# A transformer block's head and attention: last x tile on another queue, crossbar transposes, fewer fillers, a new order

## The chip, the cores and the metric

The kernel runs on one core of one Trainium2 chip. The metric is the device time of one execution in microseconds. Executions vary, so each kernel is run several times in alternation with the kernel before, on the same chip; the calls used three chips (the record's numbers 6, 8 and 14), so fast means of different calls are compared with care. An execution is called slow when it is more than 1.5% above the fastest of its kernel; verdicts use the fast ones only. The profile's span is shorter than the measured time by about 1.8 us in every run listed here (98.78 us and 97.0, 101.95 and 100.1; the extremes are 1.74 and 1.88), so spans can be compared with times once 1.8 us is added. The granted clock is the share of full speed that the profile records for TensorE. A load's landing is the moment at which its data has arrived; it is issued earlier, from the queue of an engine.

## The reference

B = 2 batches of N = 256 tokens, width D = 1152, everything in bf16:

```python
mod = (silu(c) @ w_mod).reshape(B, 6, 1, D)      # the kernel needs shift_a, scale_a, gate_a
h   = layernorm(x) * (1 + scale_a) + shift_a
q, k, v = split(h @ wqkv)
p   = softmax(q @ k.T * D ** -0.5)
out = x + gate_a * ((p @ v) @ wo)
```

## The kernel before

The 512 tokens are four x tiles of 128 rows, x0 to x3. The rows of x0 and x1 (batch 0) are transposed first and centred afterwards, with means from a matmul with ones; x2 and x3 are normalised first. Keys are computed from the scaled, not yet shifted rows as soon as the scale weights (s0 to s3, column groups of `w_mod`) and the first chunks of the key weights (w0 to w8) are there. A helper records every operation with what it reads and writes and adds the semaphores; each engine is given its operations in the order of the list. Fillers are matmuls on zeros whose results nobody uses; they are meant to keep TensorE busy at the start. The parts that the change touches:

```python
SGROUPS = [(0, 2), (2, 4), (4, 6), (6, 9)]
LOADS = [                       # all on SyncE's queue
    ('s', 0), ('w', 0, 1), ('s', 1), ('w', 1, 2), ('w', 2, 4), ('s', 2), ('w', 4, 6), ('s', 3), ('w', 6, 9),
]
WARM = 12                       # filler matmuls on zeros, 128x512, ahead of everything on TensorE
ORDER = [                       # head: the emission order of some 80 steps on all engines
    ('bn', 2, 1), ('third', 2, 0), ('cT',), ...
]
...
    op(AC, lambda e: e.dma_start(c_sb[:, :], c[:, :]), w=[("c",)], dma=True)
    load_x(SP, 2)
    load_x(AC, 3)
    load_x(SP, 0)
    load_x(AC, 1)               # the last x tile: second on ScalarE's queue
...
    def p_T(b):                 # probabilities transposed on TensorE, 4 per batch
        bank = next_bank()
        for qt in range(2):
            i = 2 * b + qt
            for sbk in range(2):
                op(PE, lambda pe, ...: pe.transpose(psb[bank][...], e_sb[:, i, sbk * P:(sbk + 1) * P], ident[:, :]), ...)
        op(DVE, lambda v: v.tensor_copy(pT_sb[:, b, :, :], psb[bank][...]), ...)
...
    v_tile(0)
    sbanks = [score(i) for i in range(TT)]
    for i in range(TT):
        softmax(i, sbanks[i])
    v_tile(1)
    ...                         # gate row, and 8 DMAs that spread it over the partitions
    v_tile(2)
    p_T(0)
    p_T(1)
    v_tile(3)
```

## Time and profile before

| | before |
|---|---|
| time, median of the first runs | 100.17 us (100.02 to 100.8, 4 runs) |
| the profiled execution | 101.95 us, span 100.1 us, mean granted clock 0.983, state slow |
| TensorE busy | 94.0 us |
| x1's landing | 8.95 us |
| first key matmul | 13.91 us |
| third set of scale matmuls (needs s3) | 22.61 us |

The second row is the one to keep in mind. The profile is of one execution, and this one was slow. The rest of the table describes that execution, not the median. The last row is this piece of its chain of waits (start, length, what), with which later runs are compared:

```profile
22.61 0.65 PE psbank L490 x27
```

### The profile page before, as it was taken

To read this page: it belongs to the slowest core of one execution; us is meant where nothing else is said; L and a number is where in the kernel's file an instruction comes from. 1 tells how busy PE (TensorE), PEld (TensorE's weight loads), DVE (VectorE), ACT (ScalarE), POOL (GpSimd) and SP (SyncE) were. 2 spreads that over 40 slices of the span, in tenths; PEclk is the share of its full clock that TensorE was granted. 3 is DMA by queue.
4 is the path that set the end of the run, shared out by engine and by line. 5 is a ranking of instruction groups with operands and counts; after the bars stand their busy time and mean duration, and the time that the engine had idled before them with its cause. 6 is when DMAs were issued, how large, how long until landed. Compare 5 with 4: busy or idle time off the path is not lost.

```text
span 100.1 us, 1901 instructions
## 1 busy us (share of the span) xinstructions
PE 94.0 (94%) x770; PEld 58.4 (58%) x776; DVE 49.2 (49%) x139; ACT 28.6 (29%) x63; POOL 12.8 (13%) x36
## 2 busy tenths in 40 slices
PE   5974989999999999999999999999999999999990
PEld 1344978855564454544445687556667865665670
DVE  1258196254199641320840246650523655799571
ACT  1854567980123200000604033351103810000000
POOL 4004363348021030210000000000000000000000
PEclk9996699999999999999999999999999999999999
DMA  2999999999999999999999910003775755221222
GB/s 31 356 329 318 358 326 340 359 327 313 351 351 346 355 322 386 385 393 388 395 388 391 369 51 0 0 0 17 27 51 45 40 45 62 80 79 39 79 79 79
DMA packets 20092, 21.65 MB, mean 216 GB/s; under 512 B 882, under 2 KB 16114, under 8 KB 20084
## 3 DMA queue, kind: packets, MB, share of 16 engines
q1 hardware_dynamic: 19792, 20.94, 72.0%
q10 hardware_dynamic: 292, 0.59, 1.6%
q8 instruction: 6, 0.10, 0.4%
q14 instruction: 2, 0.02, 0.0%
HBM read 19.76 MB, written 1.18 MB: 209 GB/s over the span
## 4 chain that ended last, share of the span: by engine, by line
PE 87%; DMA 7%; DVE 2%; ACTq 1%; issue 1%
PE psbank L542 35%; PE psbank L720 18%; PE psbank L845 18%; DMA x_sb<-in_x_dram 7%; PE psbank L807 4%; PE psbank L733 4%; PE psbank L490 3%; PE psbank L408 2%; PE psbank L392 2%; PE psbank L784 1%; ACTq L295 1%; DVE pvT_sb L521 1%; DVE nm_sb L417 0%; PE psbank L767 0%; DVE xnT_sb L426 0%
## 5 line engine op out<-in xcount | busy, mean ns | idle before, releaser
L542 PE MATMUL psbank<-pvT_sb,wq_sb 128*128 128x512 bf16 (+2 forms) x107 | 18.2, 319 | 0.3
L720 PE MATMUL psbank<-wq_sb,hT_sb 128*128 128x384 bf16 x108 | 18.2, 326 | 0.0
L542 PE MATMUL psbank<-hT_sb,wq_sb 128*128 128x512 bf16 x79 | 17.9, 379 | 0.1
L845 PE MATMUL psbank<-wm_sb,pvT_sb 128*128 128x384 bf16 x99 | 16.3, 326 | 0.0
L720 PEld LDWEIGHTS psbank<-wq_sb,hT_sb 128*128 128x128 bf16 x108 | 10.4, 98 | 7.0 <-DVE v_sb L337 0.2
L542 PEld LDWEIGHTS psbank<-pvT_sb,wq_sb 128*128 128x128 bf16 x111 | 9.7, 98 | 6.9 <-DVE pvT_sb L521 0.3
L845 PEld LDWEIGHTS psbank<-wm_sb,pvT_sb 128*128 128x128 bf16 x99 | 9.7, 98 | 6.3
L542 PEld LDWEIGHTS psbank<-hT_sb,wq_sb 128*128 128x128 bf16 x81 | 7.8, 97 | 9.1
L339 ACT ACTIVATE qkT_sb<-psbank 128x512 bf16<-128x512 f32 x8 | 4.3, 598 | 22.3 <-PE psbank L542 22.3
L337 DVE CAST qkT_sb<-psbank 128x512 bf16<-128x512 f32 x10 | 6.3, 685 | 5.6 <-PE psbank L542 5.6
L337 DVE CAST v_sb<-psbank 128x384 bf16<-128x384 f32 x6 | 3.2, 554 | 10.4 <-PE psbank L720 10.4
L858 DVE TENSOR_TENSOR ga_sb<-psbank,gate_rep 128x384 bf16<-128x384 f32 x11 | 6.1, 556 | 4.0 <-PE psbank L845 4.0
L331 PE MATMUL psbank<-warm_sb 128*128 128x512 bf16 x12 | 4.6, 568 | 1.2 <-DVE warm_sb L319 1.2
L339 ACT ACTIVATE v_sb<-psbank 128x384 bf16<-128x384 f32 x6 | 2.9, 487 | 9.8 <-PE psbank L720 9.8
L490 PEld LDWEIGHTS psbank<-scT_sb,wm_sb 128*128 128x128 bf16 x162 | 5.0, 96 | 1.0
L490 PE MATMUL psbank<-scT_sb,wm_sb 128*128 128x2 bf16 x162 | 5.0, 163 | 0.0
L484 DVE TENSOR_TENSOR hT_sb<-pvT_sb,rep_sb 128x256 bf16<-128x256 bf16 x9 | 3.2, 421 | 2.7 <-ACT rep_sb L478 2.7
L343 DVE BATCH_NORM_STATS2 stat_sb<-x_sb 128x6 f32<-128x384 bf16 x4 | 2.0, 553 | 4.4 <-DMA x_sb<-in_x_dram 4.4
L861 DVE TENSOR_TENSOR xo_sb<-x_sb,ga_sb 128x384 bf16<-128x384 bf16 x11 | 3.9, 358 | 0.4
L733 PE MATMUL psbank<-qkT_sb 128*128 128x256 bf16 x36 | 4.1, 273 | 0.0
L807 PE MATMUL psbank<-pT_sb,v_sb 128*128 128x256 bf16 x36 | 4.1, 273 | 0.0
L392 PE MATMUL psbank<-ident,x_sb 128*128 128x128 bf16 x18 | 2.0, 266 | 2.1 <-DMA x_sb<-in_x_dram 1.6
(86 smaller groups left out, 89.0 us busy)
## 6 DMA issues: line engine op xcount, KB each, us to landing
wm_sb<-in_w_mod_dram SPq DMA_DIRECT2D x4, 864.0 KB, 9.4
wq_sb<-in_wqkv_dram SPq DMA_DIRECT2D x4, 672.0 KB, 10.0
wq_sb<-in_wqkv_dram SPq DMA_DIRECT2D x3, 864.0 KB, 11.5
wm_sb<-in_w_mod_dram SPq DMA_DIRECT2D x1, 2592.0 KB, 16.5
wm_sb<-in_wo_dram SPq DMA_DIRECT2D x1, 2592.0 KB, 18.2
wm_sb<-in_w_mod_dram SPq DMA_DIRECT2D x3, 576.0 KB, 8.2
wq_sb<-in_wqkv_dram SPq DMA_DIRECT2D x2, 576.0 KB, 10.3
out_dram<-xo_sb SPq DMA_DIRECT2D x11, 96.0 KB, 1.6
```

The source lines that it names most:

```text
L331: op(PE, lambda pe: pe.matmul(ps[bank][:, 0:512], warm_sb[:, 0:P], warm_sb[:, 0:512], start=True, stop=True), r=[("warm",)], w=[("ps", bank)])
L337: op(DVE, lambda v: v.tensor_copy(dst, src), r=r, w=w)
L339: op(AC, lambda a: a.activation(dst, src, ACT.Copy), r=r, w=w)
L392: op(PE, lambda pe, cc=cc, bank=bank, lo=lo, src=src: pe.transpose(psb[bank][:, lo:lo + P], src[:, i, cc * P:(cc + 1) * P], ident[:, :]), ...
L490: op(PE, lambda pe, cc=cc, k=k: pe.matmul(ps[7][:, col + 2 * cc:col + 2 * cc + 2], src[:, k, (cc - base) * P:(cc - base + 1) * P], scT_sb[ ...
L542: op(PE, lambda pe: pe.matmul(ps[bank][:, lo:hi], wq_sb[:, k, col * P:(col + 1) * P], src[:, k, lo:hi], start=(k == 0) if start is None el ...
L720: op(PE, lambda pe, k=k, q=q, bank=bank: pe.matmul(ps[bank][:, 0:384], hT_sb[:, k, i * P:(i + 1) * P], wq_sb[:, k, 2 * D + q * 384:2 * D + ...
L733: op(PE, lambda pe, cc=cc: pe.matmul(ps[bank][:, 0:NTOK], qkT_sb[:, cc, i * P:(i + 1) * P], qkT_sb[:, DC + cc, b * NTOK:(b + 1) * NTOK], s ...
L807: op(PE, lambda pe, h=h, cc=cc, sbk=sbk: pe.matmul(ps[bank][:, h * NTOK:(h + 1) * NTOK], v_sb[:, 2 * b + sbk, cc * P:(cc + 1) * P], pT_sb[ ...
L845: op(PE, lambda pe, i=i, k=k, rhs=rhs, n=n, bank=bank: pe.matmul(ps[bank][:, 0:n], pvT_sb[:, k, i * P:(i + 1) * P], rhs, start=(k == 0), s ...
L858: op(DVE, lambda v, b=b, c0=c0, c1=c1, n=n, bank=bank, s=s: v.tensor_tensor(ga_sb[:, s, 0:n], ps[bank][:, 0:n], gate_rep[:, b, c0:c1], ALU ...
L861: op(DVE, lambda v, i=i, c0=c0, c1=c1, n=n, s=s: v.tensor_tensor(xo_sb[:, i, c0:c1], x_sb[:, i, c0:c1], ga_sb[:, s, 0:n], ALU.add), r=[("x ...
```

## The change

The intent: x1 joins the other x tiles at the front of SyncE's queue and so lands before the weights; TensorE's eight transposes of the probabilities become four crossbar DMAs; 12 fillers become 5 + 4; and the order of the head is recomputed for the new landing times.

```diff
 LOADS = [
-    ('s', 0), ('w', 0, 1), ('s', 1), ('w', 1, 2), ('w', 2, 4), ('s', 2), ('w', 4, 6), ('s', 3), ('w', 6, 9),
+    ('x', 0), ('x', 1), ('s', 0), ('s', 1), ('w', 0, 1), ('w', 1, 2), ('w', 2, 4), ('s', 2), ('w', 4, 6),
+    ('s', 3), ('w', 6, 9),
 ]
-WARM = 12
+WARM = 5
 ORDER = [
-    ('bn', 2, 1), ('third', 2, 0), ('cT',), ('third', 2, 1), ('bn', 3, 0), ('xT', 0, 1), ...
+    ('cT',), ('third', 2, 0), ('cTo',), ('bn', 2, 0), ('e1',), ('third', 2, 1), ('warm', 4), ('d1',), ...
     (the other steps, and where ('smm', 1) stands: now ahead of the first key matmul)
 ]
     load_x(SP, 2)
     load_x(AC, 3)
-    load_x(SP, 0)
-    load_x(AC, 1)
-    def p_T(b):
-        ... (four TensorE transposes and a copy)
+    def p_T(i):
+        b, qt = i // 2, i % 2
+        op(SP, lambda e: e.dma_start(pT_sb[:, b, :, qt * P:(qt + 1) * P], e_sb[:, i, :], transpose=True),
+           r=[("e", i)], w=[("pT", b, qt)], dma=True)
     for i in range(TT):
         softmax(i, sbanks[i])
+        p_T(i)
     v_tile(2)
-    p_T(0)
-    p_T(1)
```

## The prediction

> **What bounds the kernel now.** I began with the chain of waits that ends last, because it says which engine's time the end is made of.
>
> ```profile
> PE 87%; DMA 7%; DVE 2%; ACTq 1%; issue 1%
> ...
> 1.70 7.25 DMA x_sb<-in_x_dram
> 8.95 0.04 issue
> 8.99 1.14 PE psbank L392 x9
> 10.13 0.96 PE psbank L408 x9
> ...
> 13.34 0.52 DVE pvT_sb L521
> 13.86 0.05 issue
> 13.91 1.00 PE psbank L542 x10
> ...
> 71.47 0.45 PE psbank L767 x8
> ...
> 97.85 0.29 DVE xo_sb L850
> ```
>
> The columns are start, length and what. From 13.91 us, the first key matmul, to 97.8 us the chain is TensorE with gaps of at most 0.05 us. Before 13.91 it is one load, an x tile of 288 KB that takes 7.25 us, and then 4.96 us of work that this tile releases. So time can be won in two ways: let the first key matmul start earlier, provided that what it then needs is there, or take instructions off TensorE.
>
> Next I asked why that tile is late, in the DMA issues and then line by line, narrowed to one issue at a time.
>
> ```profile
> x_sb<-in_x_dram SPq DMA_DIRECT2D x2, 288.0 KB, 3.9
> x_sb<-in_x_dram ACTq DMA_DIRECT2D x2, 288.0 KB, 6.1
> ```
>
> The single issues are: x2 issued at 0.73, 3.1 us to landing (3.8); x0 1.18 + 4.8 = 6.0; x3 1.30 + 4.9 = 6.2; x1 1.70 + 7.3 = 9.0. x1 is second on ScalarE's queue, while SyncE's queue already carries the first scale weights s0 (576 KB, issued at 1.65, landed at 9.2). Further landings, needed below: the key weights w0 2.11 + 7.8 = 9.9, s1 2.78 + 8.9 = 11.7, w1 3.27 + 9.1 = 12.4, s2 7.47 + 8.2 = 15.7, s3 10.69 + 9.0 = 19.7.
>
> Last, the stretches with the granted clock, since filler matmuls are removed.
>
> ```profile
> core 0: us, PE busy (x) PEld busy (x) DVE busy (x) ACT busy (x) POOL busy (x), PEclk, DMA share, GB/s
> 1.20:5.00 3.80, 3.80 (x9) 1.32 (x10) 0.63 (x2) 2.42 (x4) 0.62 (x4) 1.00 0.82 254
> 5.00:8.40 3.40, 1.92 (x22) 1.01 (x20) 2.18 (x7) 1.96 (x10) 0.00 (x0) 1.00 1.06 333
> 8.40:11.80 3.40, 2.81 (x27) 2.81 (x28) 1.49 (x5) 1.67 (x4) 2.06 (x5) 0.51 1.08 335
> 13.90:20.70 6.80, 6.71 (x91) 5.66 (x94) 4.00 (x14) 5.36 (x10) 3.04 (x7) 1.00 1.08 348
> ```
>
> DMA runs at about 340 GB/s throughout, and TensorE's clock falls to half from 8.4 to 11.8, after a stretch in which it was busy 1.92 of 3.40 us. In that half-clock stretch a transpose or a mean matmul starts every 0.107 us (0.96 us for 9).
>
> [...]
>
> **The change, part by part.**
>
> 1. *x1 on SyncE, ahead of the weights.* Its queue becomes x2, x0, x1, s0, s1, w0; ScalarE's keeps c and x3. The four tiles are 4 x 0.295 = 1.18 MB. The stretches moved 35 KB in the second microsecond, then 212, 385, 335, 323 and 333 KB, so 1.18 MB have gone by at about 5.7 us. x0 and x3 landed about 1.3 us after their 0.885 MB had passed (4.8 against 6.0 to 6.2). With the same lag x1 lands at 7.0, 2 us earlier. The price is w0: w1 has the same bytes ahead of it as before (12.4), w0 stands 0.229 MB / 0.34 MB per us = 0.7 us ahead of w1, so 11.7 instead of 9.9, and s1 about 11.0. The first key matmul cannot start before 11.7.
>
> 2. *The new order of the head.* It has no fewer real instructions, only another order, so I walked each engine with before's durations. ScalarE: both statistics of x3 until 7.6, eviction of x0's second part 0.70 to 8.3, Ln and Exp to 8.8, eviction of x1's second part to 9.5. VectorE: eviction of x1's first part to 8.15, x2 normalised 8.85 to 9.6. TensorE: x1 transposed 7.05 to 7.6, three parts of the means, 18 scale matmuls when s0 is there (9.2), x2's transposes, the last mean. At full clock that mean ends at 10.65; then ScalarE scales it (0.3), VectorE centres (0.42) and scales (0.35), and the second 18 scale matmuls end at 11.65: first key matmul at 11.8. At half clock from 8.45 to 11.86, as in the trace of before, the last mean ends at 11.7 and the first key matmul comes at 12.85. I take the middle, 12.3.
>
> 3. *After it.* 18 scale matmuls (0.43 us) stood behind the first key matmul in before and now stand ahead of it. The block of the first four key chunks ended at 20.67, 6.76 after its start; it needs 6.3 now. So it ends at 12.3 + 6.3 = 18.6: 2.1 us gained (2.6 at full clock, 1.5 at half). Is the rest fed? s2 (15.7) is wanted at about 17.3. s3 (19.7) was wanted at 22.6 and is now wanted at about 20.1 to 20.5. Both are there; before's slack at s3, 2.9 us, is the cap of what the head can give. Later weights had over 3 us of slack.
>
> 4. *Fillers.* 12 become 5 + 4. Those cost no path time in before (the chain was waiting for x1); they matter for the clock alone.
>
> 5. *Crossbar transposes.* Eight PE transposes leave the chain: 0.45 us. Two VectorE copies (0.76 us) go too, beside other work. In their place are four DMAs of 64 KB. The last probabilities are scaled at 66.2 and the first use is at 76.1; both move earlier together. A regular small DMA here takes 4.8 to 9.2 us under a queue of eight (the gate rows) and 1.6 us alone (the stores), so about 7 us of slack should do. They stand ahead of the gate rows in SyncE's queue, which begin at 67.5.
>
> Sum: 2.1 + 0.45 = 2.55 us off 100.29 = 97.75; with full clock 2.6 + 0.45 gives 97.2, with half clock 1.5 + 0.45 gives 98.3.
>
> **Rivals.**
>
> *The clock takes the gain.* Fewer fillers leave the stretch around 5 to 8.4 emptier still (perhaps 1.5 of 3.4 us), so the half-clock stretch stays[...]. For it: before lost its clock at 1.92 of 3.40. Against: with x1 at 7.0 TensorE is nearly always busy from then on[...]. Cost: result 98.3[...].
>
> *Weights become the bound.* w0 at 11.7 replaces x1 as the last wait. For it: s1 was moved ahead of w0. It is already in my sum as the floor 11.7; if DMA order costs 0.5 us more, the result is 98.2.
>
> *The transposes stall SyncE.* If one takes 4 us to issue, the four end 4 or 5 us after the gate rows should have begun; those in before landed between 72.3 and 84.8, and the second batch's are wanted by VectorE at 87.0. That slack of 2 us would be spent, result about 99 to 101. Against: no view shows SyncE busy then; it had waited 24 us for the gate rows' source. I give it one chance in twelve.
>
> *The head is hidden anyway.* Then only 0.45 us remain: 99.8. Against: the chain of waits has no idle TensorE after 13.91 that could absorb an earlier start.
>
> **Range and chances.** The two clock cases give 97.2 and 98.3, and x1's landing is uncertain by 0.4 us; that makes 96.9 to 98.9, with 97.8 in the middle, rounded towards the half-clock case. The 2% mark is at 98.3, right at the unlucky clock case, so faster by over 2% gets 0.66, within 2% 0.30, slower by over 2% 0.04 for stalled transposes.
>
> **What would show it.** Right: x1's landing about 7 us; the first key matmul between 11.8 and 12.9 with its last wait on VectorE's scaling or on w0; the fourth chunk's end near 18.6; no PE group for the probabilities' transposes, and the product with v following the last v tile without a gap. Wrong: a wait of TensorE on a weight DMA near 15 to 20 us; a granted clock of 0.5 after 12 us; TensorE idle ahead of the product with v, or VectorE waiting for the gate rows.

## The result and the profile after

The changed kernel took 98.81 us in the median (98.78 to 99.07, 4 runs) against 100.17 us: 1.4% less, inside the stated range by 0.1 us (it ends at 98.9), but 1.0 us above the predicted 97.8. The outcome held likeliest, faster by over 2% (0.66), did not come; within 2% had been given 0.30. Six more executions of this kernel (e5) had a median of 99.1 us, just above the range. Ratios in this document are the mean time of one kernel's fast runs over the mean of the other's fast runs of the same rounds, so they are not quite the ratios of the medians. Here the ratio is 0.9859, with a 95% interval of 0.9812 to 0.9905. Every experiment is marked correct on record, among them e5, which is this kernel.

The chain of waits of the changed kernel (start, length, what):

```profile
PE 77%; DMA 10%; SPq 9%; issue 1%; DVE 0%
...
9.91 9.79 DMA wm_sb<-in_w_mod_dram
19.69 0.05 issue
19.74 0.83 PE psbank L492 x27
20.57 3.04 PE psbank L544 x14
...
64.28 8.88 PE psbank L722 x54
...
94.70 0.29 DVE xo_sb L843
```

The x tile is gone from the chain. In its place stands the load of the last scale weights, s3, issued at 9.91 and landed at 19.69, and the matmuls that wait for it begin at 19.74. From there on the chain is TensorE without a gap, as before. The two v tiles that the probabilities' transposes used to separate are one piece of 8.88 us. The last instruction begins at 94.70.

TensorE's own stretches in the head (columns as in the prediction):

```profile
core 0: us, PE busy (x) PEld busy (x) DVE busy (x) ACT busy (x) POOL busy (x), PEclk, DMA share, GB/s
1.20:4.60 3.40, 3.40 (x17) 1.16 (x18) 0.83 (x3) 2.02 (x5) 0.62 (x4) 1.00 0.79 232
4.60:8.00 3.40, 2.42 (x29) 1.61 (x28) 2.60 (x8) 2.94 (x10) 0.44 (x2) 1.00 1.08 336
8.00:11.20 3.20, 2.82 (x67) 2.53 (x65) 2.47 (x8) 2.29 (x7) 2.29 (x4) 1.00 1.12 332
```

No stretch has a granted clock of 0.5 any more, and the pace agrees: a transpose of x takes 219 ns in the median, while in the first trace the slow ones took up to 314. And the DMA issues (KB, then us to landing), with one line of the timeline of TensorE:

```profile
x_sb<-in_x_dram SPq DMA_DIRECT2D x3, 288.0 KB, 4.4
x_sb<-in_x_dram ACTq DMA_DIRECT2D x1, 288.0 KB, 4.4
pT_sb<-e_sb SPq DMA_TRANSPOSE x4, 2.3
11.21 5.19 PE L544 MATMUL psbank<-pvT_sb,wq_sb 128*128 128x256 bf16 x47
```

x1, issued third at 1.66, needed 4.7 us and landed at 6.3. A crossbar transpose lands in 2.3 us. The first key matmul starts at 11.21.

| | before, profiled (slow) | changed, profiled (fast) |
|---|---|---|
| x1 lands | 8.95 | 6.3 |
| first key matmul | 13.91 | 11.21 |
| third scale matmuls | 22.61 | 19.74 |
| span | 100.1 | 97.0 |
| time of that execution | 101.95 | 98.78 |

Trace against trace the change gains 3.1 us, which is even more than predicted. Time against time it gains 1.4 us. The experiments had to explain that difference first.

### The profile page after: what moved, and what is told of

It is laid out like the page before. It is cut to its first block, busy times and chain, and to the rows that moved or that the text cites. A ratio compares the mean times of both kernels' runs of the same rounds, so it can differ in the third digit from the quotient of the medians.

```text
span 97.0 us, 1884 instructions
## 1 busy us (share of the span) xinstructions
PE 91.5 (94%) x759; PEld 56.1 (58%) x765; DVE 48.0 (50%) x136; ACT 28.4 (29%) x64; POOL 12.8 (13%) x36
## 3 DMA queue, kind: packets, MB, share of 16 engines
HBM read 19.76 MB, written 1.18 MB: 216 GB/s over the span
## 4 chain that ended last, share of the span: by engine, by line
PE 77%; DMA 10%; SPq 9%; issue 1%; DVE 0%
PE psbank L544 28%; PE psbank L722 18%; PE psbank L838 18%; DMA wm_sb<-in_w_mod_dram 10%; SPq L294 6%; PE psbank L735 4%; PE psbank L800 4%; PE psbank L492 3%; SPq L287 2%; SPq L283 1%; PE psbank L779 1%; PE psbank L475 0%; DVE xo_sb L843 0%
## 5 line engine op out<-in xcount | busy, mean ns | idle before, releaser
L339 DVE CAST v_sb<-psbank 128x384 bf16<-128x384 f32 x6 | 3.2, 556 | 11.8 <-PE psbank L722 11.8
L525 POOL TENSOR_SCALAR pvT_sb<-xnT_sb,s_sb 128x256 bf16<-128x256 bf16 (+1 forms) x9 | 5.1, 579 | 2.5 <-DVE s_sb L503 2.2
L333 PE MATMUL psbank<-warm_sb 128*128 128x512 bf16 x9 | 3.8, 576 | 1.2 <-DVE warm_sb L321 1.2
L735 PEld LDWEIGHTS psbank<-qkT_sb 128*128 128x128 bf16 x36 | 3.5, 98 | 0.5
```

Source lines behind the costliest of these rows:

```text
L339: op(DVE, lambda v: v.tensor_copy(dst, src), r=r, w=w)
L525: op(POOL, lambda g: g.tensor_scalar(dst, src, sc, 0.0, op0=ALU.mult, op1=ALU.add), r=rk, w=wk)
L735: op(PE, lambda pe, cc=cc: pe.matmul(ps[bank][:, 0:NTOK], qkT_sb[:, cc, i * P:(i + 1) * P], qkT_sb[:, DC + cc, b * NTOK:(b + 1) * NTOK], s ...
```

## The experiments

Theory A: the trace of before is of an execution with 3.4 us at half clock in the head, the timed ones have none, and between fast executions the head is worth about 0.9 us and the transposes 0.45. Theory B: the trace was representative, and the gain is lost after the head. The other theories stand with their runs. For each kernel the fast mean and the number of executions at a low granted clock (mean below 0.99) are given. Fast is judged by the time alone, so a few fast executions have a low clock: one each in e5 and e6, three of the six in e12.

| run | ratio (95%) | fast mean, us | low-clock executions |
|---|---|---|---|
| before, all runs of all calls | 1 | 100.22 | 30 of 132 |
| e1 before again | 1.0022 (0.9984 to 1.0060) | 100.44 | 4 of 14 |
| e2 transposes only | 0.9955 (0.9925 to 0.9986) | 99.80 | 6 of 22 |
| e3 head only | 0.9934 (0.9906 to 0.9962) | 99.67 | 2 of 22 |
| e4 x1's queue only | 0.9955 (0.9931 to 0.9978) | 99.79 | 0 of 21 |
| e5 changed kernel again | 0.9875 (0.9821 to 0.9929) | 99.21 | 1 of 6 |
| e6 changed, s3 split | 0.9996 (0.9972 to 1.0021) | 100.20 | 2 of 22 |
| e7 changed, 1 filler | 0.9897 (0.9851 to 0.9944) | 99.55 | 0 of 6 |
| e8 changed, 12 fillers | 0.9929 (0.9894 to 0.9964) | 99.65 | 1 of 14 |
| e9 old order, x1, transposes, 9 fillers | 0.9892 (0.9849 to 0.9935) | 99.34 | 0 of 6 |
| e10 changed, s3 earlier | 0.9845 (0.9800 to 0.9891) | 98.88 | 0 of 6 |
| e11 before, 1 filler | 1.0118 (1.0072 to 1.0164) | 101.59 | 0 of 6 (see there) |
| e12 new order and fillers, old loads | 1.0028 (0.9989 to 1.0066) | 100.39 | 10 of 15 |

### e1_before_again

No edit.

> The kernel before, unchanged, for a profile of a fast execution. Theory A (the profile of before that I read was of a slow execution, 101.95 us, in which the TensorE clock was at half for 3.4 us of the head; the timed fast ones have no such stretch): span about 98.2 us, mean granted clock 0.99 or more, execution time 1.8 us above the span, first key matmul near 12.2 instead of 13.91. Theory B (the profile was representative and the gain of the change was lost after the head): span about 100.1, clock 0.98, first key matmul near 13.9. Ratio to before 1.00 in both.

The profiled execution was a fast one (101.04 us, span 99.2, clock 1.0). From its chain of waits and its stretches:

```profile
1.70 7.48 DMA x_sb<-in_x_dram
...
13.02 1.00 PE psbank L542 x10
...
21.72 0.65 PE psbank L490 x27
5.00:8.40 3.40, 1.46 (x20) 0.79 (x18) 2.82 (x8) 2.11 (x10) 0.52 (x2) 1.00 1.00 308
8.40:11.80 3.40, 2.52 (x49) 2.35 (x50) 1.25 (x5) 1.80 (x4) 1.55 (x4) 1.00 1.11 341
```

x1 lands even later than in the first trace (9.18), and still the first key matmul comes 0.9 us earlier, because the stretch from 8.4 to 11.8 has full clock: 49 matmuls against 27 in the stretch of the first trace. The list of executions gives the general picture. Of 132 executions of before in all calls, 102 have a clock of 0.99 or more and 30 a clock of 0.983 or 0.966; the 30 take 101.80 us in the mean, the fast ones 100.22. So the first trace was of the rarer kind, 1.6 us longer. Theory A stands. Its number for the span, 98.2, holds for the typical fast execution (98.4 is 100.22 less 1.8); the one that was profiled was 0.8 us above that, with a first key matmul at 13.02 where 12.2 was expected. e2's trace is nearer to the typical one.

### e2_pT_only

```diff
 # the kernel before, with the changed kernel's p_T(i) after each softmax(i)
-    p_T(0)
-    p_T(1)
```

> The kernel before with only the transposes of the probabilities moved to crossbar DMA. Theory A: eight TensorE transposes leave the path, 0.45 us, ratio 0.9955 (99.7 us of 100.17). Theory B (this part is where the gain was lost, by SyncE or by the gate rows that stand behind it): ratio 1.00 or above, and the product with v or the last stage starting after a wait.

Measured: 0.9955, just as theory A said; 0.45% of 100.2 us is 0.45 us (by the interval, 0.14 to 0.75). The trace shows no wait in front of the product with v. Low-clock executions are as frequent as in before (6 of 22): this part does not touch the head.

The profiled execution was fast (99.99 us, clock 1.0), so its head is a fast head in the old order. From its chain:

```profile
1.72 6.87 DMA x_sb<-in_x_dram
...
12.42 1.00 PE psbank L542 x10
...
21.12 0.65 PE psbank L490 x27
```

The third scale matmuls come 1.5 us earlier than in the first trace (22.61). From x1's landing (8.59) to the first key matmul it takes 3.83 us here and 3.84 us in e1 (9.18 to 13.02), but 4.96 us in the first trace: half clock cost 1.1 us there, and 0.4 us is x1's later landing. Compared with the changed kernel's trace (19.74) they come 1.4 us later, and the execution took 1.2 us longer. So between fast traces the head's gain is found again in the time, and half of the 2.9 us first read from the traces was what the slow execution had lost.

### e3_head_only

```diff
 # the changed kernel, with the old p_T(b) between v_tile(2) and v_tile(3)
```

> The changed kernel with the probabilities transposed on TensorE as before, so only the loads, the fillers and the head's order are changed. Theory A: the changed kernel plus 0.45 us, 99.25 us, ratio 0.991: the head is worth 0.9 us between fast executions. Theory B: the head alone gives 2 us or more, ratio 0.98 or less.

Measured: 0.9934, or 0.66 us, a little less than theory A's 0.9 (0.991 lies inside the interval) and far from theory B's 2 us. Times e2's 0.9955 this gives 0.989; the whole change measured 0.9859 and 0.9875, with intervals that contain it. Between fast executions the parts add up, and nothing is lost after the head. Theory B falls.

### e4_x1_only

```diff
     load_x(SP, 0)
-    load_x(AC, 1)
+    load_x(SP, 1)
```

> The kernel before with one edit: x1 is the third load on SyncE's queue. x1 should land near 6.3 us as in the changed kernel. Theory C (x1's landing was the head's bound, the rest follows from it): most of the head's gain, ratio 0.992 to 0.995. Theory D (the new order is what turns the landing into an earlier first key matmul): ratio 0.998 or above.

Measured: 0.9955. One word of the source gives 0.45 us of the head's 0.66, and not one execution in 21 lost its clock. x1 landed at 6.1. What bounds it now, from its chain of waits and a stretch:

```profile
1.19 4.95 PE psbank L331 x12
...
11.33 1.00 PE psbank L542 x10
5.00:8.40 3.40, 3.17 (x38) 1.99 (x37) 2.71 (x8) 2.39 (x10) 0.21 (x1) 1.00 1.04 317
```

The chain begins with the 12 fillers: with x0 and x1 there early they are in the way. And TensorE is busy for 3.17 of the 3.40 us in which it was busy 1.92 before. The ratio lies just above theory C's range (0.992 to 0.995), which its interval covers, and theory D's 0.998 lies just outside the interval, so theory C is what this supports. The intervals of e3 and e4 overlap, so this run alone does not say what order and fillers add. Nor does it separate the queue from the place in the order: with x1 third on SyncE's queue, s0 was issued at 2.10 us, behind x1, instead of 1.65, beside it. No run left x1 on ScalarE's queue and only held the weights back.

### e5_after_again

No edit to the changed kernel.

> The changed kernel again, with more executions. Theory A: fast executions 0.987 to 0.990 of before (0.9955 of the crossbar part times 0.9934 of the head is 0.989), and no slow execution with a granted clock of 0.983, of which before has one in three.

Measured: 0.9875, inside the expected band; one execution of six (100.06 us) had a clock of 0.983. With the first four runs that is 1 of 10, against 30 of 132; ten executions are too few to tell these apart. "No slow execution" was too strong.

### e6_after_split

```diff
-SGROUPS = [(0, 2), (2, 4), (4, 6), (6, 9)]
+SGROUPS = [(0, 2), (2, 4), (4, 6), (6, 7), (7, 9)]
-    ... ('s', 2), ('w', 4, 6), ('s', 3), ('w', 6, 9),
+    ... ('s', 2), ('w', 4, 5), ('s', 3), ('w', 5, 6), ('w', 6, 7), ('s', 4), ('w', 7, 9),
```

> The changed kernel with the last scale weights split (one chunk, then two) and loaded in the order in which TensorE wants them. Theory S (in the changed kernel the landing of s3, near 19.7 to 20.0 us, is what the head waits for): no wait of TensorE on a weight DMA near 19 to 20 us, the third scale matmuls begin near 19.3, 0.3 to 0.5 us less than the changed kernel, ratio to before about 0.984. Rival (the TensorE work behind the first key matmul sets the pace and the wait is a coincidence of 0.1 us): same as the changed kernel within 0.1 us.

A miss: 0.9996, a whole microsecond lost where 0.3 to 0.5 were to be gained, and neither theory had that. What TensorE waited for in it (total us, times, longest):

```profile
PE psbank L544 <- POOL pvT_sb L525: 0.7, 2, 0.5
PE psbank L475 <- DVE s_sb L503: 0.3, 1, 0.3
```

The first is the scaling of the next key chunk on GpSimd, which in this order stands behind five small GpSimd operations for batch 0's statistics. The second is a wait for VectorE to read the scale results from the PSUM bank that the following matmuls use too. As far as this one trace tells, splitting the group put such steps closer together than TensorE's work between them could cover. The experiment moved more than the landing, so it doesn't test theory S; e10 was built to do that. (One execution of 22 took 123.0 us at a clock of 0.765; it is left out as slow.)

### e7_after_1_filler and e8_after_12_fillers

```diff
-WARM = 5
+WARM = 1          # e7; e8: WARM = 12
-    ('warm', 4),  # both
```

> The changed kernel with 1 filler matmul instead of 9. Theory F (it is x1's early landing that keeps TensorE busy enough for its clock): clock 0.99 or more in nearly all executions, time as the changed kernel within 0.3 us. Theory G (the fillers are what wins the full clock): every execution spends at least one stretch of 3.4 us of the head at half clock, mean clock 0.983 or less, 1 to 1.6 us slower than the changed kernel.

> The changed kernel with all 12 fillers of before up front. In the run with x1 alone the 12 fillers ended near 6.1 us, after x0 had landed (5.3), and stood in the chain. Theory H (the reduction of fillers is itself a gain): first key matmul 0.3 to 0.6 us later than with 9, time 0.3 us or more above the changed kernel. Theory S (the landing of s3 caps the head anyway): time within 0.2 us of the changed kernel.

With one filler: 0.9897, 0.3 us above the changed kernel by the fast means (99.55 against 99.21), not the 1 to 1.6 us of theory G. Part of that may be a late landing of s3 (20.7 in the profiled execution). One execution of the six took 101.38 us at a recorded clock of 1.0 and is left out as slow. But theory F's claim on the clock is not shown. These are the transposes of x in e7 and, below, in the changed kernel (duration in ns as min/median/max, then first and last start in us):

```profile
L394 PE MATMUL psbank<-ident,x_sb x18: 264/311/311, 5.3 to 7.1; 128*128 128x128 bf16 x18
L394 PE MATMUL psbank<-ident,x_sb x18: 217/219/230, 5.7 to 6.8; 128*128 128x128 bf16 x18
```

They start 0.107 us apart in e7, the pace of the half-clock stretch in the first trace of before, although e7's mean granted clock is 1.0 (e11 shows the same). What theory G had right is the stretch at that pace; what it had wrong is the cost. In e7 the first scale matmuls begin at 8.91, without a wait; in e5, at full pace, they begin at 8.95, after a wait of 0.8 us. The time lost at half pace falls into that wait. With twelve fillers: 0.9929, 0.4 us above, and the fillers head the chain once more:

```profile
1.19 4.71 PE psbank L333 x12
...
12.56 5.05 PE psbank L544 x48
```

The first key block comes at 12.56 in the chain, 0.9 us later than in that of e5 (11.65). That is the side of theory H, with a larger delay than it expected. The 0.4 us in the time is likely but not settled, since the intervals of e5 and e8 overlap. The prediction had counted nothing for the fillers.

### e9_x1_pT_9_fillers

```diff
 # the kernel before (old order), with three edits
-WARM = 12
+WARM = 9
-    load_x(AC, 1)
+    load_x(SP, 1)
 # and the crossbar transposes as in e2
```

> The kernel before, in its old order of the head, with three edits: x1 third on SyncE's queue, the crossbar transposes, and 9 fillers instead of 12 so that they end near 5.2 us, about when x0 lands. Theory J (the recomputed order itself is worth little; queue, fillers and transposes make the gain): ratio 0.985 to 0.989, as the changed kernel or below; first key matmul near 10.8. Theory D (the new order is needed): 0.991, the product of x1 alone and the transposes alone, or above.

Measured: 0.9892, between the two theories and overlapping the changed kernel's intervals. The recomputed order is therefore worth between nothing and some tenths of a microsecond; these runs don't resolve it. The chain of the profiled execution:

```profile
10.51 10.10 DMA wm_sb<-in_w_mod_dram
20.61 0.05 issue
```

It waited for s3 until 20.61 although its first key matmul was at 11.2 (10.8 was expected). The load ahead of s3 had taken 9.6 us to land here (in e7 too) against 7.8 us in the changed kernel's trace. What delays the load stream by up to 1.5 us in some executions was not found.

### e10_after_s3_earlier

```diff
-    ... ('s', 2), ('w', 4, 6), ('s', 3), ('w', 6, 9),
+    ... ('s', 2), ('w', 4, 5), ('s', 3), ('w', 5, 6), ('w', 6, 9),
```

> The changed kernel with one edit in the loads: the last scale weights go ahead of the second of the chunks 4 and 5, with no group split. s3 should land about 0.65 us earlier. Theory S (its landing costs the head up to 0.3 us in some executions): 0.1 to 0.3 us less than the changed kernel, ratio 0.985, no wait of TensorE on a weight DMA near 19 to 20 us. Rival (the landing and TensorE's own work are level by then): within 0.1 us of the changed kernel.

Measured: 0.9845, the lowest of the study, with a fast mean of 98.88 us; the verdict at the 2% mark is unclear. That is where theory S expected it, but its interval (0.9800 to 0.9891) overlaps those of the changed kernel, and the changed kernel's first four runs have the same mean (98.87). s3 landed at 19.2 in its trace, and the third scale matmuls began at 19.73, released by TensorE's own work. In e5's trace, without the edit, s3 also landed at 19.2, and they began at 19.79. TensorE's wait for s3 was 0.3 us in the changed kernel's first trace, 0.8 us in e7's and 0.7 us in e9's, and none in those of e4, e5, e8 and e10. So where the load is late the wait costs some tenths of a microsecond, and in other executions nothing. This version has the lowest time of those tried; that it is faster than the changed kernel is not shown.

### e11_before_1_filler

```diff
-WARM = 12
+WARM = 1
```

> The kernel before with 1 filler instead of 12. Theory F2 (with x1 late the fillers are needed to reach full clock before x1's block): the block behind x1 begins at half clock in most executions, first key matmul 13.5 or later, 1 to 1.6 us slower than fast executions of before, ratio 1.01 to 1.016. Rival (fillers do nothing): ratio 1.00.

Measured: 1.0118, 101.59 us in the fast mean, and the fastest of its executions (101.15) is above every full-clock mean. Theory F2 stands. From its chain, and from a stretch:

```profile
8.40 1.14 PE psbank L392 x9
...
13.47 1.00 PE psbank L542 x10
8.40:11.50 3.10, 3.10 (x30) 3.10 (x31) 0.85 (x3) 1.77 (x3) 1.48 (x3) 1.00 1.04 332
```

Nine transposes take 1.14 us, exactly as in the half-clock stretch of the first trace of before, but the column of the granted clock says 1.00. The chain keeps about this pace until 11.82 (means: nine in 0.96 us, then nine in 0.89), and the column says 1.00 from 11.6 to 13.4 as well. It is so in the first trace of before, too: the fillers between 1.2 and 5.0 us took 0.42 us each, against 0.22 us for a key matmul of the same 128x512 later, and the column says 1.00, while for the later loss, from 8.4 to 11.8, it says 0.51. So a mean clock of 1.0 is no proof of full clock in the head. The pace of equal matmuls is: 0.107 us a piece in such stretches, while in e8's chain, at full clock, five means took 0.28 us, or 0.056 each.

### e12_order_only

```diff
 # the kernel before, with the new ORDER and WARM = 5; loads and p_T as before
```

> The kernel before with the new order of the head and its 5 + 4 fillers, but the old loads (x1 second on ScalarE's queue, landing near 9 us) and the old transposes on TensorE. Theory C (x1's landing is what the gain hangs on, the new order is worth little without it): ratio 0.998 to 1.006, x1's wait of about 2 us in front of TensorE, and slow executions at a granted clock of 0.983 as often as in before or more often. Theory D (the order carries the gain by itself): 0.994 or below.

Measured: 1.0028 between fast executions, and 10 of 15 executions at a low clock, so the median of all is 101.83 us. Its waits and stretches:

```profile
PE psbank L393 <- DMA x_sb<-in_x_dram: 2.9, 1, 2.9
5.00:9.40 4.40, 1.51 (x14) 1.00 (x13) 2.03 (x6) 2.67 (x9) 1.58 (x4) 1.00 1.05 320
9.40:12.80 3.40, 3.40 (x48) 3.40 (x47) 1.43 (x4) 1.13 (x3) 0.02 (x1) 0.50 1.10 337
```

TensorE waits 2.9 us for a late x1, and after that idle stretch the clock is at half for 3.4 us. Over all executions the mean is 101.5 us, against 100.3 for before in the same rounds, where 3 of 20 had a low clock. Without x1 on SyncE's queue the new order with its fillers is harmful, and theory C stands. Which of the two makes the loss more frequent is not shown: the order came with 5 + 4 fillers instead of 12, and in e1 the old order waited 2.7 us for x1 and kept its clock.

## Why the prediction was right or wrong, point by point

**The base of the sum: the step that failed.** "Sum: 2.1 + 0.45 = 2.55 us off 100.29" took a difference against the first trace and subtracted it from the median of other executions (of the three timed by then; with the fourth it is 100.17). That trace was of an execution of 101.95 us, and the record of the runs said so; the prediction didn't look. Its 13.91 and 20.67 us contain 1.1 us of half clock, which e1's and e2's traces don't have, and x1's landing 0.4 us later than e2's. Between fast executions the head is worth 0.66 us (e3), not 2.1. The 3.1 us of the two traces less the 1.6 us by which low-clock executions of before are longer (101.80 less 100.22) leaves 1.5, and 1.36 was measured.

That 98.81 lies in the range is luck. The changed kernel ran its head at full clock from the transposes of x on (219 ns each), and for that case the prediction's own sum gives 97.2; the 1.6 us above it are as much as the slow base was too long. Two things hid this. The 97.8 carries half of an allowance for a half clock that did not come, and the range is not quite its own sum: 97.2 less 0.4 and 98.3 plus 0.4 make 96.8 to 98.7, not 96.9 to 98.9, and 98.81 is outside the former.

**The clock.** The prediction treated half clock as a risk of the changed kernel and took "the middle" of two cases for it alone. A half-clock stretch behind a poorly used one is what the first trace (busy 1.92 of 3.40 us, then a clock of 0.51) and e12's (1.51 of 4.40, then 0.50) show, but the prediction expected it on the wrong side. With x1 on SyncE's queue 6 of 107 executions, of all such kernels together, show a loss of the clock; before shows it in 30 of 132. (A start at half pace with a mean clock of 1.0, as in e7, is not in these counts.) An early x1 closes the idle stretch (e4: 3.17 of 3.40 us busy, 0 of 21), and a late x1 behind the new order and fillers opens it (e12: 1.51 of 4.40, 10 of 15). A share alone doesn't decide: e1 was busy for 1.46 of the same 3.40 us and kept its clock. What else decides was not shown. Over all executions an early x1 is therefore worth slightly more than the fast ones show: 3 of those 107 took over 101 us, against 32 of 132.

**x1's landing and the first key matmul.** Predicted 7.0 and, at full clock, 11.8. Measured 6.3 and 11.2 to 11.6 in two traces. In the changed kernel's stretches the 1.18 MB have passed at about 5.6 us, as predicted (5.7), so it is the lag between the bytes' passing and the landing that was over-estimated: 0.7 us, not 1.3. Issued at about the same time (1.70 and 1.66 us), x1 landed after 7.3 us with s0 issued beside it (x1 second on ScalarE's queue) and after 4.7 us with s0 issued behind it, at 2.13 (x1 third on SyncE's); no run separates the queue from the place.

**The weights as the next bound.** s3's landing was named as the cap of the head, 2.9 us against the first trace. The changed kernel's first trace hits it (22.61 to 19.74 is 2.87 us). It was named as a margin and then left out of the sum, and against a fast execution it is much nearer: from e2's 21.12 to a landing at 19.7 it is 1.4 us. "Both are there" failed for s3. It was wanted at 19.45, not at 20.1 to 20.5, and landed at 19.69; this wait of 0.3 us is one of the signs of being wrong that the prediction lists. w0 (11.1, where 11.7 was predicted) landed just ahead of the first key matmul, as said.

**The fillers.** "They matter for the clock alone" was wrong: once x0 and x1 are early, 12 of them delay the first key matmul (by 0.9 us in e8's trace), at a cost of about 0.4 us that the intervals do not settle. With the late x1 they were needed (e11, 1.2% slower without).

**The transposes.** 0.45 us, as predicted (e2). Each, of 128x256 in bf16 within SBUF, held SyncE for about 1.2 us and landed after 2.3 us, while a store of 96 KB landed after 1.6 us and an x load held SyncE for about 0.4 us. No run has a regular copy of the same bytes to compare. The gate rows started at 64.77 instead of 67.47, in step with TensorE; the stall that the prediction gave one chance in twelve did not occur.

**What stays open.** Whether x1's queue or only its place ahead of the weights matters, how much the fillers are worth in the new order (e8 against e5), what the new order adds by itself once x1 is early (e9 against e5), whether e10 is faster than the changed kernel, and what delays the load stream by up to 1.5 us near 16 to 20 us in some executions.

## What to carry to other kernels

Before working out a gain from a trace, compare that execution's own time with the median: a trace of a slow execution contains lost time that the timed ones don't have, and a saving read from it can be twice the real one (here 3.1 us against 1.4). A load that the head waits for is worth moving ahead of the bulk; here that one line gave about two thirds of the head's gain (0.45 of 0.66 us, with overlapping intervals), and none of its 21 executions lost the clock. Fillers and order are tuned to landing times: change those and the old tuning can get in the way (e8: first key matmul 0.9 us later), while the new tuning with the old landing times is worse than nothing (e12: 101.5 us in the mean over all executions, against 100.3).
